# First hundred calls of a hand-ordered attention and MLP kernel in another order, and its filler pieces at another place

## The chip, the cores and the metric

The kernel runs on one core of a Trainium2 chip. Times are device microseconds of one execution; where several runs were timed, their median is given. A profile describes one execution of its own, whose span (first to last instruction) is a little shorter than its time.

## The reference

```python
def _attn_ref(q, k, v, sort_net):        # q, k, v: (4, 8, 768, 64); sort_net: (4, 8, 8, 8)
    P = sort_net
    for _ in range(5):                   # balancing
        P = exp(P - max(P, -1))
        P = P / (sum(P, -1) + 1e-9)
        P = P / (sum(P, -2) + 1e-9)
    k_sorted = einsum('bhij,bhjcd->bhicd', P, k_b)     # 8 blocks of 96 positions
    v_sorted = einsum('bhij,bhjcd->bhicd', P, v_b)
    scores = q_b @ k_sorted^T / 8                      # within each block
    return softmax(scores) @ v_sorted
x = attention output as (3072, 512)
h = x @ w_in                                           # 512 -> 2048
out = (h * cos(h)) @ w_out                             # 2048 -> 512
```

## The kernel before, in words

The work is cut into eight chunks n = 0 to 7, each a half (four blocks of 96 positions) of one of the four batches, with all eight heads. A *unit* (n, u) is one block u = 0 to 3 of a chunk. After the balancing, all calls stand in a list that was written out by hand, `PLAN`. It is read line by line, and each engine executes its own instructions in that order. A letter at the end of a line names the engine that copies (A = ScalarE, V = VectorE) or the PSUM pool (`B` = `big`, three buffers of two banks; `c` = `acc`, two of one bank). A further number is an argument of the call.

The calls that matter here:

- `kp t` (TensorE) makes a third of the sorted keys of the first batch, `kpe t` copies it to SBUF.
- `v0 z` (TensorE) makes an eighth of the sorted values of the first batch (8 of 64 columns), `v0e z` copies it. Groups 0 to 3 read v as it was loaded. Groups 4 to 7 read `vperm`, a copy in another layout, which `vp 32` makes on GpSimd in two instructions of 16 columns each. A product's weights are 128 columns wide where only 96 are needed, so the last product of a 16-column part also reads the beginning of the next part.
- `S n u` (TensorE) makes a unit's scores, `M` takes the maximum, `X` subtracts it (both VectorE), `E` takes the exponential (ScalarE), `TP` transposes it on TensorE, `TE` copies the transpose, `AV` multiplies by the values (TensorE), `N` divides by the sum (VectorE), `XP`/`XE` transpose the result and copy it to `xT`. `QP`/`QE` turn q for the next chunk.
- `U4 h g part`, `C4`, `G4` are the first matmul of the MLP, the cosine and the product for the first chunk, cut by halves of the columns (h = 0 needs units 0 and 1, h = 1 needs 2 and 3). `U n f`, `C`, `G` do the same for later chunks; a third number in `U n f 1` makes the second of its two column groups in two half matmuls each instead of whole ones. `D`, `O`, `W` are the second matmul, the copy and the store.
- `Lw` loads w_out, `Lk` and `Lv` load k and v of the second batch; `kxp`, `z_turned`, `pk2`, `ones` are small GpSimd work.

Ahead of `PLAN` stand the loads, all issued by GpSimd (q of chunk 0 at line 1004, then k of batch 0 at 1005, v of batch 0 at 1006), and the five rounds of the balancing (`normalize`, on VectorE and ScalarE). During these TensorE turns q (`q_twice`, 64 transposes) and otherwise computes *zero products*: `keep_warm` multiplies a zero matrix into a PSUM buffer that is overwritten later. There are 15 of these at the start, then 2, 6, 2 and 4, and some in `PLAN`: where `kp` or `v0` has a last number (`kp 0 B 1`, `v0 0 B 2`), 512 columns each; in `TP` and `AV` of chunk 0, 256 columns each. The first cuts, as many as `MORE` says, divide such a product into up to four pieces along its columns; each piece is an instruction pair of its own (weight load and matmul).

A PSUM buffer is given to a call when the calls that read its former content have been listed; the call then waits for these.

Of the kernel before, what the change touches and what calls it, by code (L numbers as in the profile page):

```python
# [13 lines left out]
ALU = mybir.AluOpType  # L14
AX = mybir.AxisListType

MORE = 70
PLAN = """\
vp 32
kp 0 B 1  # L20
spv
kp 2 B 1
kpe 0 A
kp 1 B
kpe 2 V
v0 3 c 1
kpe 1 A
v0 1 c 1
v0e 3 V
S 0 0 B  # L30
v0e 1 A
v0 4 B 1
M 0 0
v0 5 c 1
Lw 0
Lw 1
v0e 4 A
Lw 2
Lw 3
ones 0  # L40
S 0 1 B
X 0 0
v0e 5 A
v0 6 c 1
M 0 1
E 0 0 0
v0 7 B
S 0 3 B
v0e 6 A
X 0 1  # L50
TP 0 0 c
v0e 7 A
M 0 3
v0 2 c
E 0 1 1
S 0 2 B
X 0 3
kxp 1
v0e 2 A
v0 0 B 2  # L60
TE 0 0 A
M 0 2
kxp 2
v0e 0 A
TP 0 1 c
X 0 2
kxp 0
z_turned 1
E 0 3 2
AV 0 0  # L70
TE 0 1 V
E 0 2 0
TP 0 3 c
N 0 0
Lk 1
AV 0 1
Lv 1
pk2
TE 0 3 A
TP 0 2 B  # L80
N 0 1
XP 0 0 B
TE 0 2 A
QP 1 1 c
XP 0 1 c
QE 1 1 0 V
z_vperm
XE 0 0 A
AV 0 3
AV 0 2  # L90
XE 0 1 V
N 0 3
U4 0 0 0
U4 0 0 1
N 0 2
z_turned 0
p_pads
U4 0 1 0
C4 0 0
QE 1 1 1 V  # L100
U4 0 1 1
G4 0 0
XP 0 3 c
XP 0 2 c
C4 0 1
U4 0 3 0
XE 0 2 V
U4 0 3 1
XE 0 3 A
G4 0 1  # L110
U4 1 2 0
C4 0 3
U4 1 3 0
G4 0 3
U4 1 2 1
U4 1 3 1
C4 1 2
U4 1 1 0
C4 1 3
G4 1 2  # L120
U4 1 1 1
bl2 c
G4 1 3
C4 1 1
U4 0 2 0
U4 0 2 1
sp2
# [260 lines left out]
G 2 5  # L388
kg 11 c
kge 11 A  # L390
U 2 6
S 3 2 c 1
C 2 6
M 3 2 1
# [438 lines left out]
def kernel(  # L833
# [16 lines left out]
    B, H, S, D = q.shape  # L850
# [197 lines left out]
    nc.scalar.activation(early[:], half_pi[:], AF.Exp)  # L1048


    pieces = [MORE]

    def keep_warm(times, t, cols=512):
        for _ in range(times):
            n = 1 + min(3, pieces[0])
            pieces[0] -= n - 1
            for i in range(n):
                c = slice(i * cols // n, (i + 1) * cols // n)
                nc.tensor.matmul(  # L1059
                    t[:, c], warm[:], warm[:, :1].to_broadcast([128, c.stop - c.start]),  # L1060
                    start=True, stop=True)

    keep_warm(15, big.tile([128, 512], FP32, name="idle", tag="big"))


    V, A = nc.vector, nc.scalar
# [31 lines left out]
    E, Q = E_eps[:, :, :nb], Q_eps[:, :nb]  # L1098
# [45 lines left out]
    def idle(times):  # L1144
        keep_warm(times, acc.tile([128, 512], FP32, name="idle", tag="acc"))

    for it in range(5):
        nc.scalar.activation(E, less[:], AF.Exp)
        if it == 0:
            nc.vector.reduce_sum(  # L1150
                maskp.rearrange("p (b e x) -> p b x e", b=2, e=2),
                ident.rearrange("p (b x e j) -> p b x e j", b=2, e=2, j=nb), axis=AX.X)
            A.copy(
                order.rearrange("k (p r) -> k p r", r=QR),
                ident[:blk, :blk].rearrange("k (r p) -> k p r", r=QR))
            q_twice(0)
            q_twice(1)
            keep_warm(2, big.tile([128, 512], FP32, name="idle", tag="big"))
        if it >= 2:
            q_place(it - 2)  # L1160
            if it < 4:
                idle((6, 2)[it - 2])
                q_twice(it)
            else:
                idle(4)
                q_place(3)
        normalize(it, (less if it < 4 else sorted_by)[:])
        if it == 1:
            nc.gpsimd.tensor_copy(held[:B * H], over[2][:, :1])
            for z in range(3):  # L1170
                load_w_in(z)
        if it == 3:
            nc.gpsimd.tensor_copy(held[:B * H], over[3][:, :1])
            load_w_in(3)
            load_q(1)
# [439 lines left out]
    def spv():  # L1615
# [3 lines left out]
        kp=kp, kpe=kpe, kxp=kxp, ks=ks, kse=kse, kg=kg, kge=kge, kswap=kswap, v0=v0, v0e=v0e,  # L1619
# [3 lines left out]
        vp=vp, vp2=vp2, vq=vq, z_vperm=z_vperm, p_pads=p_pads, pk2=pk2, bl2=bl2, sp2=sp2, spv=spv,  # L1623
        ones=ones, z_turned=z_turned, zeros=zeros_between)
    words = {"A": (A,), "V": (V,), "B": (big, "big"), "c": (acc, "acc"), "-": (None,)}
    for line in PLAN.split("\n"):
        name, *args = line.split()
        given = []
        for a in args:
            given += words.get(a) or ((int(a),) if a.isdigit() else (a,))  # L1630
        calls[name](*given)
# [42 lines left out]
```

## Time and profile before

| | |
|---|---|
| median of 3 runs | 236.35 us (236.2 to 237.87) |
| the profiled execution | 236.52 us |
| its span | 234.7 us |
| TensorE (PE) busy | 227.7 us, 97% |
| VectorE (DVE), ScalarE (ACT), GpSimd (POOL) busy | 175.2, 149.1, 93.7 us |
| DMA traffic | 31.01 MB, mean 132 GB/s |
| chain that ended last: PE, DMA | 84%, 7% of the span |

In the profile, PE is TensorE's matmuls and PEld its weight loads. A row of the timeline gives start, length, engine, source line, operation, output and inputs with their shapes, the number of instructions merged into it, and in brackets how long the engine sat idle before it and who released it. A matmul's recorded length includes its way through the array, so matmuls that follow each other overlap. The chain of waits goes back from the last instruction, at each step to what released it. A row of a stretch gives each engine's busy time and, as (xN), the number of its instructions, then the granted TensorE clock, the share of the DMA engines and GB/s.

### The profile page before, as it was taken

What the parts mean: (1) busy time and instruction counts of PE and PEld (TensorE: products, weight loads), DVE (VectorE), ACT (ScalarE), POOL (GpSimd) and SP (SyncE); (2) the same over time, 40 slices, a digit from 0 to 9 for tenths busy, and PEclk for the clock granted to TensorE, in tenths of its full rate; (3) what the DMA queues carried; (4) which work ended last, traced back from release to release, by engine and by line L of the source; (5) the groups of instructions that cost most, each with busy time, mean ns of one, the idle gap of its engine ahead of it and who ended that gap; (6) DMA issues with size and microseconds to landing.
All of it is one profiled execution on the core that took longest, in us unless ns stands there. A gap on an engine that the chain in (4) does not pass through costs nothing.

```text
span 234.7 us, 5734 instructions
## 1 busy us (share of the span) xinstructions
PE 227.7 (97%) x2380; PEld 151.0 (64%) x2380; DVE 175.2 (75%) x291; ACT 149.1 (64%) x198; POOL 93.7 (40%) x117
## 2 busy tenths in 40 slices
PE   8898999999999999999999999999999999999994
PEld 8766799657765566655666558655555596456553
DVE  5757987798898776897778977899487879455530
ACT  3365976657869859883788747666667376526511
POOL 7659998596990095972709000800000000000000
PEclk9999999999999999999999999999999999999999
DMA  5999999796699779996999668953943650341003
GB/s 63 223 195 207 204 207 226 128 216 164 134 102 179 167 138 168 99 218 152 127 158 95 86 104 148 210 83 68 162 159 64 82 175 3 66 125 47 0 0 134
DMA packets 66841, 31.01 MB, mean 132 GB/s; under 512 B 55552, under 2 KB 62336, under 8 KB 66560
## 3 DMA queue, kind: packets, MB, share of 16 engines
q0 software_dynamic: 24048, 13.64, 43.6%
q1 hardware_dynamic: 42480, 16.83, 34.1%
q8 instruction: 18, 0.29, 0.5%
q10 hardware_dynamic: 288, 0.20, 0.3%
q14 instruction: 7, 0.06, 0.1%
HBM read 27.27 MB, written 6.29 MB: 143 GB/s over the span
## 4 chain that ended last, share of the span: by engine, by line
PE 84%; DMA 7%; ACT 3%; POOL 3%; issue 1%; DVE 1%; DVEq 0%; POOLq 0%
PE o L1544 32%; PE h L1499 30%; DMA kv<-in_v_dram 6%; PE h L1522 5%; PE av L1430 3%; POOL vperm L993 2%; PE sc L1320 2%; PE ks L1201 2%; PE xps L1469 2%; PE o L1638 2%; DMA kv<-p_buf 1%; PE vs L1257 1%; PE pps L1406 1%; PE vs L1292 1%; PE sc L1347 1%
## 5 line engine op out<-in xcount | busy, mean ns | idle before, releaser
L1544 PE MATMUL o<-w_out_t,gg 128*128 128x512 bf16 x368 | 87.2, 379 | 0.0
L1499 PE MATMUL h<-xT,w_in_t 128*128 128x384 bf16 (+1 forms) x516 | 78.2, 305 | 0.0
L1511 DVE TENSOR_TENSOR gg<-c,h 128x768 bf16<-128x768 f32 x56 | 53.0, 949 | 19.0 <-ACT c L1505 18.9
L1505 ACT ACTIVATE c<-h,half_pi 128x768 f32<-128x768 f32 x56 | 50.4, 901 | 22.0 <-PE h L1499 20.7
L1499 PEld LDWEIGHTS <-w_in_t 128*128 128x128 bf16 x516 | 47.1, 98 | 22.4 <-DVE xT L1072 0.2
L1544 PEld LDWEIGHTS <-gg 128*128 128x128 bf16 x368 | 33.3, 98 | 33.7 <-DVE gg L1511 0.6
L1379 ACT ACTIVATE p_buf<-s 96x768 bf16<-96x768 f32 x32 | 26.4, 841 | 12.1 <-DVE s L1375 8.0
L1361 DVE TENSOR_REDUCE mx<-sc 96x8 f32<-96x768 f32 (+1 forms) x41 | 31.5, 772 | 3.3 <-PE sc L1333 1.4
L993 POOL COPY vperm<-kv 64x1536 bf16<-64x1536 bf16 (+1 forms) x10 | 28.1, 2853 | 2.5 <-DMA kv<-in_v_dram 2.5
L1375 DVE TENSOR_TENSOR s<-sc,mx 96x384 f32<-96x384 f32 (+1 forms) x33 | 24.1, 733 | 1.2
L1447 DVE TENSOR_TENSOR xn<-av,r 96x512 bf16<-96x512 f32 x32 | 22.0, 687 | 1.1
L943 POOL DMA_DIRECT2D kv<-in_q_dram x24 | 16.0, 681 | 0.8 <-issue 0.5
L1446 DVE RECIPROCAL r<-av 96x8 f32<-96x8 f32 x32 | 6.3, 198 | 8.1 <-PE av L1430 8.0
L1070 ACT CAST kTs<-ks 128x512 bf16<-128x512 f32 (+1 forms) x18 | 11.0, 632 | 2.2 <-PE ks L1201 2.2
L1070 ACT COPY xT<-xps 128x384 bf16<-128x384 bf16 x10 | 4.8, 476 | 11.3 <-PE xps L1469 11.3
L943 POOL DMA_DIRECT2D q_mem<-in_q_dram x16 | 10.7, 685 | 2.8 <-DMA kv<-in_v_dram 2.4
L1070 ACT COPY kv<-o 128x512 f32<-128x512 f32 (+2 forms) x10 | 5.3, 529 | 9.6 <-PE o L1544 7.0
L1059 PEld LDWEIGHTS <-warm 128*128 128x128 bf16 x116 | 9.8, 119 | 2.3 <-DVE half_pi L1042 1.0
L1522 PE MATMUL h<-xT,w_in_t 128*128 128x192 bf16 x128 | 11.1, 246 | 0.0
L1059 PE MATMUL idle<-warm 128*128 128x128 bf16 (+2 forms) x99 | 9.7, 273 | 1.3 <-DVE half_pi L1042 1.0
L1522 PEld LDWEIGHTS <-w_in_t 128*128 128x128 bf16 x128 | 10.4, 98 | 0.0
L1567 POOL CAST held<-q_turned 96x1 f32<-96x1 bf16 x2 | 0.4, 182 | 24.4 <-DMA q_turned<-q_mem 17.0
(120 smaller groups left out, 276.4 us busy)
## 6 DMA issues: line engine op xcount, KB each, us to landing
out_dram<-kv SPq DMA_DIRECT2D x12, 256.0 KB, 2.5
out_dram<-o_s SPq DMA_DIRECT2D x10, 256.0 KB, 3.3
w_in_t<-in_moe_w_in_dram POOLq DMA_DIRECT2D x4, 512.0 KB, 12.4
w_out_t<-in_moe_w_out_dram POOLq DMA_DIRECT2D x4, 512.0 KB, 11.6
kv<-in_k_dram POOLq DMA_DIRECT2D x2, 768.0 KB, 10.0
kv<-in_v_dram POOLq DMA_DIRECT2D x2, 768.0 KB, 13.6
pair<-in_k_dram POOLq DMA_DIRECT2D x2, 768.0 KB, 10.3
kv<-in_v_dram POOLq DMA_DIRECT2D x6, 256.0 KB, 6.1
```

Source lines behind the costliest of these rows:

```text
L943: nc.gpsimd.dma_start(out=q_heads[:, i, :, e], in_=src[:, ih * IC + i, :, e])
L993: nc.gpsimd.tensor_copy(dst, src)
L1070: eng.copy(dst, src)
L1361: nc.vector.reduce_max(mx[:], s_view(n, u, hp), axis=AX.XY if n < 2 else AX.X)
L1375: nc.vector.tensor_tensor(s, sc, mx.to_broadcast(list(s.shape)), op=ALU.subtract)
L1379: nc.scalar.activation(p[:, :, :blk], s_t.pop((n, u)).rearrange("p e h c -> p (e h) c"), AF.Exp, scale=scale)
L1447: nc.vector.tensor_tensor(xn.rearrange("p h e d -> p e h d")[:, e], avv[:, :, :, :D], r[:, e].to_broadcast([blk, e.stop - e.start, H2, D]) ...
L1499: nc.tensor.matmul(o[:, f2, x * w:(x + 1) * w], w_in_t[:, kk, f * 128:(f + 1) * 128], xT[n][:, kk, x * w:(x + 1) * w], start=(kk == 0), st ...
L1505: nc.scalar.activation(c[:], ps["h", n, fp][:, :, :TC], AF.Sin, bias=half_pi[:, 0:1])
L1511: nc.vector.tensor_tensor(gt[n, fp // 2][:, f:f + 2], ps.pop(("c", n, fp))[:], ps.pop(("h", n, fp))[:, :, :TC], op=ALU.mult)
L1522: nc.tensor.matmul(o[:, part, f2 * w:(f2 + 1) * w], w_in_t[:, kk, f * 128:(f + 1) * 128], xT[0][:, kk, h * w:(h + 1) * w], start=(kk == 0) ...
L1544: nc.tensor.matmul(out_ps[n, ts][:], gt[n, q][:, f % 4, ts * 128:(ts + 1) * 128], w_out_t[:, f, :], start=(f == 0), stop=(f == FC - 1))
```

## The change

The first hundred lines of `PLAN` are put into another order. Two zero products are dropped (`kp 2`, `v0 4`), `v0 4` moves directly behind `v0 3`, the scores of units 0 and 1 move ahead of `v0 1` and `v0 5`. `AV 0 2` comes ahead of `AV 0 3`, `XP 0 3` between two parts of `U4`, and some C4 and G4 change places. One later line, `U 2 6`, is split. The number of cuts `MORE` becomes two numbers: 18 before and during the balancing, 52 from the start of `PLAN`; a zero product of 512 columns is now cut into up to five pieces, one of 256 into up to three.

```diff
-MORE = 70
+MORE = 18,52
 PLAN = """\
-vp 32
 kp 0 B 1
 spv
-kp 2 B 1
+kp 2 B
+kp 1 B
+vp 32
 kpe 0 A
-kp 1 B
+v0 3 c 1
+v0 4 B
+kpe 1 A
 kpe 2 V
-v0 3 c 1
-kpe 1 A
+S 0 0 B
+v0e 3 V
 v0 1 c 1
-v0e 3 V
-S 0 0 B
+v0e 4 A
+S 0 1 B
 v0e 1 A
-v0 4 B 1
+Lw 0
 M 0 0
+X 0 0
 v0 5 c 1
-Lw 0
+E 0 0 0
 Lw 1
-v0e 4 A
 Lw 2
 Lw 3
+S 0 3 B
+v0e 5 A
 ones 0
-S 0 1 B
-X 0 0
-v0e 5 A
+M 0 1
 v0 6 c 1
-M 0 1
-E 0 0 0
+v0e 6 A
 v0 7 B
-S 0 3 B
-v0e 6 A
 X 0 1
-TP 0 0 c
 v0e 7 A
 M 0 3
+E 0 1 1
 v0 2 c
-E 0 1 1
 S 0 2 B
-X 0 3
 kxp 1
+TP 0 0 c
 v0e 2 A
 v0 0 B 2
 TE 0 0 A
+v0e 0 A
+X 0 3
 M 0 2
...
 TE 0 2 A
 QP 1 1 c
+QE 1 1 0 V
+XP 0 0 B
+XE 0 0 A
 XP 0 1 c
-QE 1 1 0 V
 z_vperm
-XE 0 0 A
+XE 0 1 V
+AV 0 2
+N 0 2
 AV 0 3
-AV 0 2
-XE 0 1 V
-N 0 3
+z_turned 0
 U4 0 0 0
 U4 0 0 1
-N 0 2
-z_turned 0
+C4 0 0
 p_pads
+N 0 3
 U4 0 1 0
-C4 0 0
 QE 1 1 1 V
+XP 0 3 c
+G4 0 0
 U4 0 1 1
-G4 0 0
-XP 0 3 c
+C4 0 1
 XP 0 2 c
-C4 0 1
+XE 0 2 V
 U4 0 3 0
-XE 0 2 V
 U4 0 3 1
+G4 0 1
 XE 0 3 A
-G4 0 1
 U4 1 2 0
+U4 1 3 0
 C4 0 3
-U4 1 3 0
+U4 1 2 1
...
-U 2 6
+U 2 6 1
...
-    pieces = [MORE]
+    pieces = [MORE[0]]
 
     def keep_warm(times, t, cols=512):
         for _ in range(times):
-            n = 1 + min(3, pieces[0])
+            n = min(1 + pieces[0], max(3, cols // 102))
             pieces[0] -= n - 1
...
     words = {"A": (A,), "V": (V,), "B": (big, "big"), "c": (acc, "acc"), "-": (None,)}
+    pieces[0] = MORE[1]
     for line in PLAN.split("\n"):
```

More of the change, by code (lines that the diff above doesn't have):

```diff
@@ L61 @@
 TE 0 0 A
+v0e 0 A
+X 0 3
 M 0 2
+E 0 3 2
 kxp 2
-v0e 0 A
+kxp 0
 TP 0 1 c
 X 0 2
-kxp 0
+AV 0 0
 z_turned 1
-E 0 3 2
-AV 0 0
 TE 0 1 V
@@ L73 @@
 TP 0 3 c
+Lk 1
+Lv 1
 N 0 0
-Lk 1
 AV 0 1
-Lv 1
+N 0 1
 pk2
@@ L80 @@
 TP 0 2 B
-N 0 1
-XP 0 0 B
 TE 0 2 A
 QP 1 1 c
+QE 1 1 0 V
+XP 0 0 B
+XE 0 0 A
 XP 0 1 c
-QE 1 1 0 V
 z_vperm
-XE 0 0 A
+XE 0 1 V
+AV 0 2
+N 0 2
 AV 0 3
-AV 0 2
-XE 0 1 V
-N 0 3
+z_turned 0
 U4 0 0 0
 U4 0 0 1
-N 0 2
-z_turned 0
+C4 0 0
 p_pads
+N 0 3
 U4 0 1 0
-C4 0 0
 QE 1 1 1 V
+XP 0 3 c
+G4 0 0
 U4 0 1 1
-G4 0 0
-XP 0 3 c
+C4 0 1
 XP 0 2 c
-C4 0 1
+XE 0 2 V
 U4 0 3 0
-XE 0 2 V
 U4 0 3 1
+G4 0 1
 XE 0 3 A
-G4 0 1
 U4 1 2 0
+U4 1 3 0
 C4 0 3
-U4 1 3 0
+U4 1 2 1
+C4 1 2
+U4 1 3 1
+C4 1 3
 G4 0 3
-U4 1 2 1
-U4 1 3 1
-C4 1 2
 U4 1 1 0
-C4 1 3
+U4 1 1 1
+C4 1 1
+bl2 c
 G4 1 2
-U4 1 1 1
-bl2 c
 G4 1 3
-C4 1 1
 U4 0 2 0
```

## The prediction

> **What bounds the kernel now.** I read the page first, then the chain of waits in order of time, then the instructions of single engines around the changed calls.
>
> ```profile
> span 234.7 us, 5734 instructions
> ...
> PE 227.7 (97%) x2380; PEld 151.0 (64%) x2380; DVE 175.2 (75%) x291; ACT 149.1 (64%) x198; POOL 93.7 (40%) x117
> ...
> PEclk9999999999999999999999999999999999999999
> ```
>
> TensorE (PE) is busy for 97% of the span and its granted clock never shows less than 9 tenths. Once it streams, only less work or an earlier start can help. The chain of waits (start, us, what) says where the start is set:
>
> ```profile
> 2.74 12.95 DMA kv<-in_v_dram
> 15.74 5.55 POOL vperm L993 x2
> 21.34 0.20 PE vs L1257
> 21.54 0.22 PE sc L1333 x14
> ...
> 25.42 0.87 PE vs L1257 x8
> 26.32 0.58 ACT vS L1070
> 26.90 0.75 ACT p_buf L1379
> 27.69 0.56 PE pps L1406 x8
> ...
> 30.61 0.26 PE av L1430 x8
> 30.87 2.68 PE h L1522 x32
> ...
> 98.16 1.30 PE h L1499 x8
> ```
>
> The load of v lands at 2.74 + 12.95 = 15.69. GpSimd's two copies `vp 32` run until 21.29, and from there the chain passes through the last product of `v0 5`, the scores, `v0 0`, its copy, two exponentials and transposes to the first matmul of the MLP, `U4 0 0 0`, at about 30.75. Behind that TensorE is nearly gapless to the end, so what the kernel gains or loses is what that start gains or loses. What stands around it on TensorE:
>
> ```profile
> 14.21 0.39 PE L1059 MATMUL ks<-warm 128*128 128x512 bf16 x1
> 14.54 0.64 PE L1201 MATMUL ks<-bd,kv 64*128 64x64 bf16 x16
> 15.11 0.39 PE L1059 MATMUL ks<-warm 128*128 128x512 bf16 x1
> 15.43 1.10 PE L1201 MATMUL ks<-bd,kv 64*128 64x64 bf16 x32
> 16.46 0.39 PE L1059 MATMUL vs<-warm 128*128 128x512 bf16 x1
> 16.79 0.91 PE L1257 MATMUL vs<-bdv,kv 64*128 64x192 bf16 x8
> ...
> 19.02 0.39 PE L1059 MATMUL vs<-warm 128*128 128x512 bf16 x1
> 19.34 0.59 PE L1257 MATMUL vs<-bdv,vperm 64*128 64x128 bf16 x8
> 19.86 0.39 PE L1059 MATMUL vs<-warm 128*128 128x512 bf16 x1
> 20.18 0.56 PE L1257 MATMUL vs<-bdv,vperm 64*128 64x128 bf16 x7
> 21.34 0.20 PE L1257 MATMUL vs<-bdv,vperm 64*128 64x64 bf16 x1 [0.59 <-POOL vperm L993]
> ```
>
> The eighth product of `v0 5` waits for the second copy (its 128 columns reach into it), and the scores `S 0 1` are queued behind it in TensorE's order. VectorE and ScalarE pay for that:
>
> ```profile
> 19.13 0.95 DVE L1361 TENSOR_REDUCE mx<-sc 96x8 f32<-96x768 f32 x1 [0.71 <-PE sc L1333]
> 20.12 0.95 DVE L1371 TENSOR_TENSOR s<-sc,mx 96x768 f32<-96x768 f32 x1
> 21.81 0.95 DVE L1361 TENSOR_REDUCE mx<-sc 96x8 f32<-96x768 f32 x1 [0.74 <-PE sc L1333]
> ...
> 26.58 0.95 DVE L1371 TENSOR_TENSOR s<-sc,mx 96x768 f32<-96x768 f32 x1
> ...
> 30.26 0.34 DVE L1072 COPY xT<-xps 128x384 bf16<-128x384 bf16 x1
> ```
>
> From `M 0 1` at 21.81 VectorE runs almost without a gap to `XE 0 1`, which ends at 30.60 and is one of the two things that `U4 0 0 0` waits for. The other is the transpose copy `TE 0 2` on ScalarE: behind it `AV 0 3` and `AV 0 2` still run, in the chain to 30.87.
>
> **Why v lands at 15.69.** These are rows of the DMA-queue view: the whole span, then 11.5 to 12.6, 13.15 to 13.6 and 13.6 to 14.2. The last fence has the busy time of the engines up to 11.6 and from there to 19.3.
>
> ```profile
> q8 instruction: 18, 0.29, 0.5%
> ```
> ```profile
> q8 instruction: 1, 0.02, 5.4%
> ```
> ```profile
> DMA packets 38, 0.03 MB, mean 73 GB/s; under 512 B 6, under 2 KB 38, under 8 KB 38
> ```
> ```profile
> DMA packets 108, 0.12 MB, mean 193 GB/s; under 512 B 6, under 2 KB 107, under 8 KB 107
> ```
> ```profile
> 0.00:11.60 11.60, 9.60 (x143) 9.07 (x143) 7.41 (x34) 4.22 (x9) 8.43 (x18) 1.00 0.82 143
> 11.60:19.30 7.70, 7.45 (x124) 5.17 (x121) 3.94 (x12) 4.06 (x6) 5.22 (x5) 1.00 1.14 198
> ```
>
> Queue q8 carries 18 packets of 0.29 MB / 18 = 16 KB. Against 2 x 2380 instructions of TensorE that is one packet for about 256: these are fetches of its program. The first comes between 11.5 and 12.6, when 286 instructions have run, the second at 19.3 after 531. It takes 5.4% of 16 engines for 1.1 us, so 0.95 us of one engine. At that time all 16 engines stream k and v, whose packets are the only ones over 8 KB. Of those none starts from 13.15 to 13.6, and exactly one starts after 13.6 (108 less 107). I read this as the engine that had to fetch, with its last piece of v late. The landing waits for it.
>
> **The change, part by part.**
>
> *Pieces.* Before, 70 cuts go to the first products: 60 fills, then 8, 24, 3 and 4 during the balancing, 99 in all. Now it is 4 x 5 + 3 + 10 = 33, then 2, 6, 2, 4, in all 47. The columns are the same, and those phases wait for a load or for VectorE, so their length costs nothing. But with 64 transposes of q, TensorE now issues 2 x (47 + 64) = 222 instructions before the matmuls of `block`, 254 after them, 286 in the middle of `kp 0`. The fetch therefore starts between about 14.1 and 14.9, not 11.6, when every piece of v has begun. The landing of v gains at least 13.60 - 13.15 = 0.45 and at most the fetch's 0.95 (at worst nothing: a rival). I take 0.75: v lands at 14.94, `vp 32` runs 14.99 to 20.54, its first copy to 17.77. [...]
>
> *Fills.* Two are gone, those of `kp 2` and `v0 4`. A fill takes 0.32 to the next product (14.21 to 14.54) and 0.12 to get going behind 64-row products (15.43 + 1.10 less 0.20 for the last one's own length, then 16.46), so some 0.4 each. Seven remaining 512-column fills become five pieces: 0 to 0.06 each; I take 0.02. The 256-column ones stay as long. `U 2 6 1` makes eight half matmuls out of four: 2.68 / 32 = 0.084 each against 1.30 / 8 = 0.163 for a whole one, so 0.02 in all.
>
> *The order on TensorE*, with product times from the rows above. `kp 0` as before to 15.03; `kp 2` and `kp 1` directly behind it to 15.96 (16.37 before); fill and `v0 3` to 17.1. Now `v0 4` stands here and waits for the first copy, 17.77 + 0.06 = 17.83: 0.7 idle, in which `S 0 0` is held although its keys are ready at about 17.2. Then: `v0 4` 0.40, `S 0 0` 0.23, fill 0.46, `v0 1` 0.69, `S 0 1` 0.27, fill 0.46, `v0 5` 0.40. This is 20.74, past the second copy's 20.54, so `v0 5` waits no more. Then `S 0 3` 0.23, fill and `v0 6` 0.86, `v0 7` 0.42, `v0 2` 0.78, `S 0 2` 0.38 (it takes a buffer that `v0e 7` frees), `TP 0 0` with fill 0.55, two fills and `v0 0` 1.33. The last product of `v0 0` starts at 25.3; before it started at 26.06 (the chain's 25.42 + 0.87, less drain). That is 0.8 gained.
>
> *VectorE.* `M 0 0` starts 0.23 behind `S 0 0`, at 18.7 (19.13), `X 0 0` at 19.7, `M 0 1` at 20.55 directly behind it instead of 21.81, and the row of equal operations follows 1.2 earlier up to `X 0 2`. *ScalarE* limits: `v0e 0` starts with the 0.8 gained, then `E 0 3`, `E 0 2`, `TE 0 3` and `TE 0 2` follow at their old durations. `AV 0 2` now goes first, with its fill already run while it waits: another 0.1. `U4 0 0 0` starts 0.9 earlier, at 29.85; `XE 0 1`, 1.05 earlier, is no longer late.
>
> *Behind it.* `XP 0 3` moves between two U4 parts and takes a buffer that `XE 0 1` has freed; its `N 0 3` ends some 0.4 before. `U4 1 3 0` ahead of `C4 0 3`, and the exchanged C4/G4, leave TensorE fed: each C4 waits for its own U4 part alone. On GpSimd and SP nothing changes order, and no queue is passed: the `Lw` issues follow `vp 32` as before. The q load's issue on GpSimd, and its time to landing from the DMA-queue view between 12.6 and 14.2:
>
> ```profile
> 12.85 0.79 POOL L933 DMA_DIRECT2D q_mem<-in_q_dram  x1
> ...
> q_mem<-in_q_dram POOLq DMA_DIRECT2D x1, 384.0 KB, 14.8
> ```
>
> The loads that queue up on GpSimd are paced by the DMA engines and land as before. The nearest is the q of `QP 1 1`: issued at 12.85, it lands 14.8 later at 27.65, and `QP 1 1` now starts at 28.2 (29.2 before), still 0.5 behind it. Sum: -0.9 at `U4`, +0.02 for `U 2 6 1`: **-0.9 us**. The profiled execution took 236.52 (span 234.7 and 1.8 around it), so it would take 235.6. The runs' median is 236.35, which gives **235.5**.
>
> **Rivals.** *The landing does not move* (the late piece of v is late for another reason, or the fetch strikes again). Then `v0 4` stands idle until 18.52 + 0.06, `S 0 0` comes 0.3 later than now, but `S 0 1` still runs ahead of `v0 5`; `v0 0` gains only 0.1 and `AV 0 2` 0.1. 236.1. For it: only one packet's lateness speaks for my reading. Against it: its size fits 0.95.
>
> *Gained and given back*: the start is early, but a later stage waits for a transfer that is not. 236.35. Against it: the chain holds 7% DMA, and nearly all of that is the first load.
>
> *The clock falls: slower than before.* The 0.7 idle, with two fills fewer, might make the gate lower the granted clock. The start shows the price, as products of 128 columns in two stretches:
>
> ```profile
> 1.00:5.90 4.90, 4.90 (x47) 1.00 0.67 77
> 5.90:6.70 0.80, 0.80 (x16) 1.00 1.66 307
> ```
>
> 9.6 per us at first, then 20: half speed for 4.9 us. Falling once while TensorE has dense work costs half of that, 2.45: 235.5 + 2.45 = **238.0**. It decides from the stall before `v0 4` onwards. Against it: 0.59 idle at 20.75 (the row of 21.34) did not move the PEclk row. [...]
>
> *The change does not do what it says.* That can only be half so: the scores stand earlier in TensorE's order whatever becomes of the fetch, and the half that can fail, the pieces, is the first rival.
>
> **How the numbers follow.** My forecast, 235.5 with a range of its own from 235.1 (v lands 0.95 earlier, and nothing else is late) to 235.9 (0.45), has 0.62. The landing that stays (236.1) has 0.16, given back (236.35) 0.11, the slower clock (238.0) 0.05, a larger gain than the sum (up to 1.5, if VectorE's whole 1.2 comes through and the pieces cost nothing: 234.8) 0.06. The range 234.8 to 236.6 leaves out the clock and little else. A measurement of this kernel can tell about 1%, 2.4 us, from no change; all but the clock's case lie within it. Faster by over 1%: 0.03; within 1%: 0.91; slower by over 1%: 0.06.
>
> **What would show it.** Right: the fetch's packet after 14; no packet over 8 KB starting after 13.6; `vperm` starting near 15.0; TensorE idle for 0.7 before `v0 4`, released by GpSimd; `M 0 1` directly behind `X 0 0`; `U4` from about 29.85, and the same distance from there to the end (234.7 - 30.75 = 203.95). Wrong: `vperm` still near 15.7 (the fetch was not the cause, then 236.1), a wait of `QP 1 1` for its load, a new wait of PE between 30 and 60, or fewer than 9 tenths in PEclk.

## The result, and the profile after

The changed kernel takes 235.29 us (median of 11 runs, 235.07 to 235.77); the kernel before took 236.4 beside it (11 runs, 235.81 to 237.87). The ratio is 0.9944, 95% interval 0.9929 to 0.9959: 1.1 to 1.3 us faster, of which the forecast of 235.5 had 0.9. The sum came out nearly right, but not by its own steps: the start gained more than predicted, and a part of that was lost again later.

The page of the profile after, which took 235.77 us, the longest of its runs:

```profile
span 234.0 us, 5701 instructions
...
PE 224.7 (96%) x2353; PEld 148.5 (63%) x2374; DVE 175.3 (75%) x291; ACT 149.1 (64%) x198; POOL 93.9 (40%) x117
...
PEclk9999999999999999999999999999999999999999
```

As before, TensorE's clock holds and it is busy nearly throughout (2353 of its 2374 matmuls were recorded). The DMA queues between 13.6 and 14.2 us, then the chain of waits (start, us, what):

```profile
DMA packets 119, 0.13 MB, mean 224 GB/s; under 512 B 3, under 2 KB 118, under 8 KB 118
...
q8 instruction: 1, 0.02, 10.1%
```
```profile
2.74 11.74 DMA kv<-in_v_dram
14.53 2.79 POOL vperm L993
17.37 0.59 PE vs L1258 x8
...
29.07 0.26 PE av L1431 x8
29.33 1.98 PE h L1523 x24
...
59.23 4.75 DMA kTs<-kTs
64.11 0.50 PE sc L1321 x8
...
102.97 3.22 DMA kv<-p_buf
106.23 0.43 PE av L1431 x8
```

The one packet over 8 KB that starts there (119 less 118) is the fetch itself: every piece of v is under way by then. v lands at 2.74 + 11.74 = 14.48, 1.21 earlier than before. The chain reaches the MLP's first matmuls at 29.33 (30.87 before, 1.54 later). Two links further down were not in the chain of before in this form: the key swap of the second batch, which now takes 4.75, and a longer `kv<-p_buf` (2.87 before). TensorE and VectorE at the places that the prediction named:

```profile
16.40 0.92 PE L1258 MATMUL vs<-bdv,kv 64*128 64x192 bf16 x8
17.37 0.51 PE L1258 MATMUL vs<-bdv,vperm 64*128 64x128 bf16 x6
...
29.17 0.50 PE L1523 MATMUL h<-xT,w_in_t 128*128 128x192 bf16 x4
```
```profile
64.11 0.50 PE L1321 MATMUL sc<-kTs,q_turned 128*128 128x96 bf16 x8 [0.52 <-DMA kTs<-kTs]
```
```profile
18.23 0.95 DVE L1362 TENSOR_REDUCE mx<-sc 96x8 f32<-96x768 f32 x1 [0.19 <-PE sc L1334]
19.22 0.95 DVE L1372 TENSOR_TENSOR s<-sc,mx 96x768 f32<-96x768 f32 x1
20.09 0.94 DVE L1362 TENSOR_REDUCE mx<-sc 96x8 f32<-96x768 f32 x1
```

`v0 4` starts at 17.37 with hardly a pause behind `v0 3` (16.40 + 0.92 is 17.32, of which the last product's own recorded length, from 17.10 on, is 0.22), `M 0 1` follows `X 0 0` without a gap at 20.09 (21.81 before), `U4 0 0 0` starts at 29.17 instead of 30.75, 1.58 earlier. But the profiled execution as a whole is only 236.52 - 235.77 = 0.75 us shorter: 0.83 us of the 1.58 is given back, and the scores behind the key swap at 64.11, before which TensorE stands for 0.52, are one place of it.

All kernels that were run, each with one profiled execution. "U4" is the first row of `h` in its chain of waits; the column behind it is the span less that start. The medians and ratios leave out executions whose mean granted clock was below 0.98 (the last column counts them; they took 241 to 245 us) but keep those of e3 and e12 with 0.986 to 0.993, save that the ratio of e12 also leaves out its slowest, of 241.34.

| kernel | v lands | U4 | U4 to end | profiled, us | median, us | ratio to before, 95% | clock < 0.98 |
|---|---|---|---|---|---|---|---|
| before | 15.69 | 30.87 | 203.9 | 236.52 | 236.3 to 236.6 | 1 | 0 |
| after | 14.48 | 29.33 | 204.6 | 235.77 | 235.29 | 0.9944 (0.9929 to 0.9959) | 0 of 11 |
| after, again (e8) | 14.11 | 29.13 | 204.2 | 235.06 | 235.06 | 0.9939 (0.9916 to 0.9961) | 0 of 6 |
| pieces alone (e1) | 13.88 | 30.21 | 204.9 | 236.9 | 236.2 | 0.9994 (0.9979 to 1.0008) | 0 of 12 |
| order alone (e2) | 15.28 | 30.03 | 204.7 | 236.52 | 236.01 | 0.9979 (0.9956 to 1.0002) | 7 of 12 |
| new order, no cuts (e3) | 13.95 | 28.93 | 209.7 | 240.38 | 237.89 | 1.0063 (1.0033 to 1.0094) | 0 of 12 |
| new order, 40 cuts ahead (e4) | 14.69 | 29.56 | 204.4 | 235.86 | 236.41 | 1.0 (0.9975 to 1.0025) | 5 of 12 |
| order alone, two fills back (e5) | 15.38 | 30.10 | 204.1 | 236.01 | 235.98 | 0.998 (0.9964 to 0.9995) | 1 of 12 |
| after without the split (e6) | 14.26 | 29.36 | 204.7 | 235.88 | 235.3 | 0.995 (0.9932 to 0.9967) | 0 of 10 |
| e3 with 15 splits (e7) | 14.20 | 28.94 | 205.3 | 236.04 | 235.38 | 0.995 (0.9931 to 0.9969) | 0 of 8 |
| after, `vperm` later (e9) | 13.90 | 29.82 | 204.7 | 236.34 | 235.92 | 0.9967 (0.9948 to 0.9987) | 4 of 12 |
| after, a `D` ahead (e10) | 14.21 | 29.13 | 205.2 | 236.1 | 234.74 | 0.992 (0.9892 to 0.9949) | 0 of 6 |
| e7 with that `D` ahead (e11) | 13.88 | 28.93 | 203.7 | 234.45 | 234.45 | 0.9903 (0.9878 to 0.9929) | 0 of 6 |
| before, no cuts (e12) | 13.97 | 30.12 | 209.5 | 241.34 | 239.55 | 1.0097 (1.0059 to 1.0135) | 0 of 6 |

### The profile page after: what moved, and what is told of

It is laid out like the page before. It is cut to its first block, busy times and chain, and to the rows that moved or that the text cites. A ratio compares the mean times of both kernels' runs of the same rounds, so it can differ in the third digit from the quotient of the medians.

```text
span 234.0 us, 5701 instructions
## 1 busy us (share of the span) xinstructions
PE 224.7 (96%) x2353; PEld 148.5 (63%) x2374; DVE 175.3 (75%) x291; ACT 149.1 (64%) x198; POOL 93.9 (40%) x117
## 4 chain that ended last, share of the span: by engine, by line
PE 80%; DMA 10%; ACT 3%; issue 2%; POOL 2%; DVE 1%; SPq 0%; DVEq 0%; ACTq 0%; POOLq 0%
PE h L1500 30%; PE o L1545 29%; DMA kv<-in_v_dram 5%; PE h L1523 5%; PE av L1431 3%; PE sc L1321 2%; DMA kTs<-kTs 2%; PE vs L1258 2%; PE o L1640 2%; PE xps L1470 2%; DMA kv<-p_buf 1%; DMA pT<-p_buf 1%; PE ks L1202 1%; POOL vperm L993 1%; PE pps L1407 1%
## 5 line engine op out<-in xcount | busy, mean ns | idle before, releaser
L1545 PE MATMUL o<-w_out_t,gg 128*128 128x512 bf16 x348 | 84.2, 379 | 1.1 <-issue 0.3
L1060 PE MATMUL idle<-warm 128*128 128x512 bf16 (+4 forms) x46 | 9.0, 364 | 2.2 <-ACT q_turned L1143 1.1
L1060 PEld LDWEIGHTS <-warm 128*128 128x128 bf16 x106 | 7.7, 111 | 5.4 <-issue 2.7
```

Of the source, the lines that this page charges most:

```text
L1545: nc.tensor.matmul(out_ps[n, ts][:], gt[n, q][:, f % 4, ts * 128:(ts + 1) * 128], w_out_t[:, f, :], start=(f == 0), stop=(f == FC - 1))
```

## The experiments

### The two halves of the change (e1, e2)

e1 keeps the old order and takes the new cuts; e2 takes the new order and split with the old cuts:

```diff
 e1, against before:                    e2, against after:
-MORE = 70                              -MORE = 18,52
+MORE = 18,52                           +MORE = 70,0
 (and the new rule for n in keep_warm,   (and the old rule for n in keep_warm)
  with the second number from PLAN on)
```

> The old order of calls and the old fills; only the cuts are as in the new kernel (18 ahead of the list, 52 in it, up to five pieces). Theory (the fetch of TensorE's program delays one sixteenth of v): the first fetch comes at about 14 instead of 11.6, v lands at 14.5 to 14.9 instead of 15.7, v0 5 waits no more for the second copy of vperm, U4 starts 0.6 to 0.8 earlier than before; with a few tenths given back later, 235.8 to 236.0. Rival (the new order does it): v lands near 15.7, 236.4 as before.

> The new order of calls and the new fills; only the cuts are as in the kernel before (70, at the first products, up to four pieces, none left for the list). Theory: the first fetch is back at about 11.6 and v lands near 15.7; TensorE idles over 1 us before v0 4, and U4 starts only 0.1 to 0.3 earlier than before: 236.1 to 236.3. Rival (the order does it): v lands near 15.7 or not, 235.3 as the new kernel.

Measured: the fetch moves with the cuts, not with the order. In e1 it comes at 14.06 and v lands at 13.88; in e2 it comes at 11.49 and v lands at 15.28, its last sixteenth 1.35 behind the fifteenth (13.93). Waits of e2, first in its chain, then on TensorE:

```profile
2.74 12.54 DMA kv<-in_v_dram
15.34 2.78 POOL vperm L993
...
30.03 1.98 PE h L1523 x24
```
```profile
18.17 0.51 PE L1258 MATMUL vs<-bdv,vperm 64*128 64x128 bf16 x6 [0.87 <-POOL vperm L993]
```

With the late landing TensorE does stand before `v0 4`, for 0.87. At U4 each half is worth something, 0.66 in e1 and 0.84 in e2, and together they make 1.50, about what the whole change shows. For e2 that is far more than the 0.1 to 0.3 expected, and the falls of the clock in seven executions (taken up at e5 and e9) were not expected. At the end neither half alone is worth it: e1's interval holds 1, e2's just does, and e1's median of 236.2 is above its expected 235.8 to 236.0. What e1 gains at the start it loses at two transfers. Its chain of waits, and the DMA view between 108.2 and 110.9 us (the digits are the busy share of the 16 DMA engines in 40 slices):

```profile
106.07 5.06 DMA pT<-p_buf
111.18 0.43 PE av L1430 x8
...
136.43 4.54 DMA xT<-xn
```
```profile
DMA  9521019888899610000000000000001000010000
...
q8 instruction: 1, 0.02, 3.7%
...
xT<-xn SPq DMA_TRANSPOSE x1, 4.3
```

A program fetch starts at 108.64, 2.57 behind the issue of a transposing transfer that is still running, lasts for 1.61 us, and from 109.3 on the DMA engines move next to nothing for 1.6 us. The transpose `pT<-p_buf` takes 5.06 where it takes 2.94 in the profile before, `xT<-xn` behind it 4.3 instead of 2.33. The same happens at 138.54 to the `xT<-xn` issued at 136.43. The kernel before has a fetch in that transfer too (at 138.45; it takes 3.84), so there e1 loses only the difference, 0.70. This gave the **theory of the fetches**: a fetch that falls into a transfer on which the chain depends makes it longer (here by 2.12 for the `pT<-p_buf`), and where it falls follows from how many instructions TensorE has been given before.

### How many cuts, and where (e3, e4)

```diff
 e3, against after:   e4, against after:
-MORE = 18,52        -MORE = 18,52
+MORE = 0,0          +MORE = 40,52
```

> The new kernel without any cut: every zero product is one instruction pair. Theory (only the number of instructions ahead of the first fetch counts): the first fetch comes at about 15, v lands at 14.5, the start of U4 and the time are those of the new kernel, 235.2 to 235.5. Rival (the cuts in the list do something of their own, for the clock or for the weight loads behind them): 0.3 or more slower than the new kernel, or fewer than 9 tenths of the clock granted.

> The new kernel with 40 cuts ahead of the list instead of 18 (55 first products instead of 33). Theory: 256 instructions have run at about 12.4, so the first fetch comes near 12.9, when the last piece of v has begun on every engine: v lands at 14.5 to 14.9 and the time is that of the new kernel within 0.2. Rival (each instruction moved behind the balancing helps a little): half way between the order alone and the new kernel, 235.7 to 235.9.

e4 misses in the fetch's place: it comes at 11.23, inside the load, not where the count of instructions put it; the landing is 14.69 and U4 at 29.56. It misses in the time too: 236.41, not that of the kernel after. Its profiled execution (235.86) is its fastest, so where the others lose more is not shown. The count tells the place of a fetch only roughly: the first one comes behind 286 instructions of TensorE in before and behind 244 in after, so that no run shows the expectation's 256 as the count at which it starts, and the eleventh one comes behind 2778 in before and behind 2708 in e1, which has as many ahead of it. e3 refutes the expectation that missing cuts cost nothing. Its start is earlier than after's (28.93 against 29.33), and it is slower than before by 0.6%. Its chain and TensorE around 105 us, then two stretches (the number behind POOL's is the granted clock):

```profile
28.93 1.98 PE h L1523 x24
...
102.04 5.83 DMA kv<-p_buf
107.91 0.65 PE av L1431 x8
108.56 5.90 PE o L1545 x16
```
```profile
104.43 0.20 PE L1348 MATMUL sc<-kTs,q_turned 64*128 64x96 bf16 x1
107.25 0.47 PE L1348 MATMUL sc<-kTs,q_turned 64*128 64x96 bf16 x7 [2.61 <-DMA kTs<-kTs]
```
```profile
104.50:107.20 2.70, 0.13 (x1) 0.03 (x1) 1.47 (x2) 0.20 (x1) 0.00 (x0) 0.88 1.23 88
107.20:108.00 0.80, 0.56 (x9) 0.35 (x9) 0.24 (x1) 0.00 (x0) 0.00 (x0) 0.50 1.11 241
```

The fetch that the kernels before and after and e1, e2 and e4 have between 94.5 and 98.6 comes at 104.34 here, in the key swap of the next batch. The swap is late, TensorE stands for 2.61 us, and its clock falls to half: the same 16 matmuls of `o` take 5.90 instead of the 3.45 to 3.46 of before and after. The fall is only a part of the loss: seven of the twelve executions keep their clock (1.0) and still take 236.9 to 238.0.

### Is it the number of instructions? (e7, e12)

If so, putting the missing instructions back at another place must cure e3, and taking the cuts out of the kernel before must spoil it. e7 splits all of `U 1 0` to `U 2 7`, 8 instructions for each split; e12 is before without cuts:

```diff
 e7, against e3:                            e12, against before:
-U 1 0                                     -MORE = 70
+U 1 0 1                                   +MORE = 0
 (and so on to U 2 7: 15 splits in all,
  U 2 6 is split already)
```

> The new order without any cuts, as in the run of 237.89, but with all of U 1 0 to U 2 7 split (15 more, 120 instructions for the 124 of the missing cuts): the start stays as early (U4 near 28.9), the program fetches from about 97 us on come where they come in the kernel after (97 to 98, 109 to 112, 137 to 138) and not at 104.3, inside the key swap. Theory of the fetches: the stall of 2.6 us at 104.5 and the fall of the clock behind it go away, no execution over 239, median 235.0 to 235.7 (start 0.24 earlier than after, splits +0.3). Rival (the cuts do something of their own, whatever the fetches do, or the early start itself is what runs into the swap): still 237 to 238, with the stall at 104 to 107.

> The kernel before, in its old order, without any cuts (70 pairs, 140 instructions fewer at the start). Theory of the fetches: the first fetch comes at about 17.5, v lands at 13.9 to 14.2 and U4 starts 0.5 to 0.8 earlier than before's 30.75; but from then on all fetches come 140 instructions later, one of them at 104 to 105 inside the key swap as in the new order without cuts, TensorE waits there for 1 to 3 us, and the time is 237 to 239, slower than before, in spite of the earlier start. Rival (that stall belongs to the new order or to its start at 28.9, not to the number of instructions): 235.5 to 236.3, and no wait of over 0.5 us at 104 to 107.

Both came out as the theory of the fetches said, and against its rivals. e7: 235.38 instead of 237.89 with the same start, and its fetch back at 98.13. e12 is slower than before by 0.97% (239.55, a little over the 237 to 239 expected) although its U4 starts 0.75 earlier; its fetch comes at 105.11. Its chain, TensorE's wait, and two stretches:

```profile
103.23 5.44 DMA kv<-p_buf
108.72 0.65 PE av L1430 x8
109.37 4.83 PE o L1544 x16
```
```profile
108.05 0.33 PE L1347 MATMUL sc<-kTs,q_turned 64*128 64x96 bf16 x7 [2.37 <-DMA kTs<-kTs]
```
```profile
108.00:110.00 2.00, 1.61 (x17) 0.92 (x17) 1.49 (x2) 0.00 (x0) 0.00 (x0) 0.65 0.97 194
110.00:112.00 2.00, 2.00 (x6) 0.76 (x5) 1.22 (x3) 0.84 (x1) 0.93 (x3) 0.50 0.59 176
```

The second part of this swap takes 6.78 in e3 and 6.81 in e12, with the fetch in it, and 5.05 to 5.70 in the twelve other profiles. That is not the whole delay: in e3 it lands 1.86 later than in e7, of which 1.09 is its length and 0.77 a later issue, whose cause is not shown.

So the cuts, of which I said that their length costs nothing, do matter, by the instructions that they add ahead of everything else.

### The split, and the kernel after again (e6, e8)

```diff
 e6, against after:
-U 2 6 1
+U 2 6
```

> The kernel after with U 2 6 unsplit: eight instructions fewer on TensorE from about 97 us on, so each later program fetch comes some 0.6 us later (111.0 to about 111.6, 137.6 to 138.2). My sum put the split at +0.02: 235.3, range 235.0 to 235.6. Theory of the fetches (where one falls into a transposing transfer that the chain waits for, 0.4 to 2.6 us are lost): the fetch near 111 stays clear of the pT and xT transfers (which end at 109.3) and so the time stays too, unless the one near 138 takes the xT transfer issued at 135.9 from off the path to on it: then 235.6 to 236.0.

> The kernel after once more, for a second profile beside the others. Theory of the fetches: where a fetch falls varies with the execution, so the wait of 0.52 us for the key swap at 64.1 (fetch at 59.23, 1.44 us long) is absent in most executions; a profile near the median of 235.3 shows U 1 without it, a swap of about 3.7 instead of 4.75, and the end 1.2 to 1.3 earlier than before's. Rival (the wait belongs to the kernel): it is there again, and the profile stands at 235.3 for another reason, found elsewhere.

The split alone moves nothing that these runs resolve (235.3 against 235.06 and 235.29). e8's execution is at the median of its six runs, and the wait of after's first profile is absent:

```profile
63.23 0.72 PE L1321 MATMUL sc<-kTs,q_turned 128*128 128x96 bf16 x8
```

The fetch came at nearly the same moment as in after (59.30 against 59.23), but lasted 0.92 and not 1.44, and the swap's second part took 3.47 instead of 4.75. All 14 profiles fall in line here: without a fetch in it (e3, e7, e11, e12) this part takes 2.98 to 3.02, with a fetch of 0.88 to 0.96 (before, e1, e4, e5, e8) 3.47 to 3.73, with one of 1.33 to 1.44 (after, e2, e6, e9, e10) 4.21 to 4.75. So this wait hangs on the execution: the 0.52 of the first profile of after is absent in the second, and in e6, e9 and e10 TensorE stands there for 0.25, 0.34 and 0.38 (in e6 released by a copy on ScalarE). Without it e8 gives back 0.28 of the 1.74 that it has at U4. Why a fetch lasts longer in one execution than in another is not shown.

### The executions in which the clock falls (e5, e9)

e5 puts the two dropped zero products back into e2; e9 makes `vperm` later in after, without another instruction on TensorE:

```diff
 e5, against e2:     e9, against after, in vp(lo):
-kp 2 B             +early = vperm[slice(0, 64), :CD].rearrange("p (d c) -> p d c", d=D)
+kp 2 B 1           +nc.gpsimd.tensor_copy(early[:, lo:lo + 5], vv[slice(0, 64), lo:lo + 5, :blk])
-v0 4 B
+v0 4 B 1
```

> The order alone with the 70 cuts as before, and the two dropped zero products back (kp 2 and v0 4): TensorE has 0.8 us more to do while it waits for vperm (idle before v0 4 0.87 us in the profile of the order alone). Theory A (the executions of the order alone that take 240.9 to 243.6, with a mean clock of 0.955 to 0.972, lose their clock in the stall before v0 4 when v lands late): the idle time there falls to about 0.1, no execution over 239, median 235.6 to 236.2. Theory B (they lose it later, where a program fetch falls into a transposing transfer that TensorE waits for, as in the run without cuts, where 2.61 us idle at 104.5 to 107.2 was followed by half the clock up to 113): the stall at the start is no matter, and between a quarter and two thirds of the executions still take 240 or more. Either way U4 starts near 30.0.

> The kernel after with the first 5 of vperm's columns copied twice, so that GpSimd's first copy is done some 0.87 us later (5/16 of 2.79) and TensorE stands idle before v0 4 for about 1.1 us instead of 0.2, as long as in the profile of the order alone (0.87); its instructions, and so its program fetches, stay as they are. Theory A (the executions of 240 and more, with a mean clock of 0.955 to 0.972, which the order alone and the forty cuts show, lose their clock in that stall): a part of the executions, 2 to 7 of 12, take 239 to 245. Theory B (they lose it elsewhere): no execution over 239. In both the others take 235.6 to 236.2, the U4 start 0.7 to 0.87 later than after's.

The counts speak for theory A on both sides: with cover the count goes from 7 of 12 to 1 of 12 (theory A said none), and a later `vperm` alone brings 4 of 12 (240.9 to 244.1) into a kernel that had none in 17. In the new order, the four kernels whose profile shows a wait before `v0 4` (0.87 in e2, 0.51 in e9, 0.26 in e4, 0.25 in e5) are the four that have such executions; the other seven had none in 59. But the counts do not follow the length of the wait (5 of 12 in e4, 1 of 12 in e5), and the waits were other than expected (about 1.1 for e9, 0.1 for e5). No execution with a fallen clock was profiled, so that the clock falls in this wait is not shown, nor why the times come in two groups (about 241 and 244); and e9 also makes GpSimd's later issues some 0.85 later than in e8.

The two fills themselves were worth little: e5's U4 starts at 30.10, e2's at 30.03, against some 0.4 for each in my sum. In front of a late `vperm` they are hidden.

### A place at which most versions pay, and a faster version (e10, e11)

Between 102 and 117 us after, e8 and e2 each lose 0.36 to 0.57 of their lead. TensorE waits there for two transfers in a row, the swap and `kv<-p_buf`; the kernel before, whose chain goes through `kv<-p_buf` too, waits for that one alone (so does e1, which loses nothing there). Before, e8, then e7:

```profile
106.97 0.43 PE L1430 MATMUL av<-vS,kv 96*128 96x65 bf16 x8 [0.34 <-DMA kv<-p_buf]
```
```profile
104.89 0.33 PE L1348 MATMUL sc<-kTs,q_turned 64*128 64x96 bf16 x7 [0.20 <-DMA kTs<-kTs]
105.51 0.43 PE L1431 MATMUL av<-vS,kv 96*128 96x65 bf16 x8 [0.30 <-DMA kv<-p_buf]
```
```profile
105.38 0.33 PE L1348 MATMUL sc<-kTs,q_turned 64*128 64x96 bf16 x7 [0.73 <-DMA kTs<-kTs]
106.04 0.43 PE L1431 MATMUL av<-vS,kv 96*128 96x65 bf16 x8 [0.33 <-DMA kv<-p_buf]
```

e10 and e11 list a part of the second matmul, which is ready, ahead of both:

```diff
+D 2 1 1
 T 4 0 B
 vge 0 8 A
 AV 3 1
 hp 3 3
 Lq 5
-D 2 1 1
```

> The kernel after with D 2 1 1 (0.86 us of TensorE) listed ahead of T 4 0 and AV 3 1, which in all the profiles wait there for the key swap and for kv<-p_buf (0.20 + 0.30 us in the second profile of after, 0.42 in that without the split): if the 0.36 us that every version gives back between 102 and 117 is that wait, the profile shows no TensorE wait there and an end that is 0.3 earlier: 234.8 (234.5 to 235.0), some 0.3 below after's 235.06 to 235.29. If the wait only moves to what follows (AV 3 2 for the pT transfer, M 4 0 which comes up to 0.4 later): 235.1 to 235.3, no change.

> The new order without cuts and with the 15 splits (235.38; it lost 0.94 between 102 and 117, with 0.74 + 0.33 us of waits for the same two transfers, and 0.5 at 140 for an xT transfer with a fetch in it), with D 2 1 1 ahead in the same way. If those waits are the loss, 0.5 to 0.8 comes back: 234.6 to 234.9, below the kernel after. If the queue's lateness is only passed on: 235.2 to 235.5.

e11 takes 234.45, 0.97% below before, with an interval that ends where e7's begins (0.9929 and 0.9931). It is the fastest kernel here, and the only one whose start comes through whole (U4 to end 203.7, 203.9 before). Of the 1.59 between the profiled executions of e7 and e11, 1.10 is won at this place, the rest between 137 and 152 us. Its chain has no transfer there any more:

```profile
28.93 1.98 PE h L1523 x24
...
104.26 0.34 PE vs L1285 x16
104.60 0.97 PE o L1545 x4
105.57 0.28 PE sc L1348 x8
105.85 0.38 PE av L1431 x8
```

e10's median of 234.74 points the same way, but its interval overlaps after's, and its profiled execution is its slowest (236.1, the others up to 234.87). There `kv<-p_buf` took 4.73, and TensorE still waits for 0.45 and 0.47, though the `D` ahead of it fills about 1.0:

```profile
106.59 0.33 PE L1348 MATMUL sc<-kTs,q_turned 64*128 64x96 bf16 x7 [0.45 <-DMA kTs<-kTs]
107.39 0.43 PE L1431 MATMUL av<-vS,kv 96*128 96x65 bf16 x8 [0.47 <-DMA kv<-p_buf]
```

## Why the prediction was right, and where it was not

**The time** was right, at 235.29 for 235.5, by two errors of opposite sign: -1.58 instead of -0.9 at U4, and +0.83 in the profile instead of nothing behind it. That they nearly cancel is luck.

**The fetch delays v.** Right, in both directions (e1, e2). It came at 14.00, just ahead of the forecast 14.1 to 14.9. The "about 256" instructions to a packet were my estimate: 4760 / 18 is 264, and in the profile before the 18 fetches start 247 instructions apart on average (188 to 319). Four profiles with the first fetch at 11.2 to 11.7 have v landing at 15.69, 15.28, 14.69 and 15.38 (mean 15.26); the ten with it at 14 or later at 13.88 to 14.48 (mean 14.08). **The size was wrong**: 1.2 and not 0.75. My upper bound, the fetch's own 0.95, was no bound: the last sixteenth lies 1.35 behind the fifteenth in e2 and in e5 (15.38 against 14.03), and why by more than the fetch lasts is not shown. The rival that the landing stays is refuted by e1.

**The order on TensorE.** The term of the idle time before `v0 4` was mis-sized: 0.7 predicted, next to none in the profile. The first copy came 0.45 earlier than I had it (17.32 against 17.77), and `v0 3` ended at 17.32 and not at 17.1. `M 0 0` at 18.23 and `M 0 1` at 20.09 are both 0.46 to 0.47 ahead of the forecast, and the step that `M 0 1` follows `X 0 0` directly held. To U4 it grows to 0.68 (29.17 against 29.85). Whether the dropped fills are worth 0.4 each no run tells: e5 has them in front of a late `vperm`, where they are hidden.

**"Nothing is given back"** is the step that failed. I held U4's distance to the end for constant, because the chain of before was nearly all TensorE there. That meant only that most transfers came just in time: 1.5 us earlier, the swaps and `kv<-p_buf` come last. At one place even that was not so, for `kv<-p_buf` stands in the chain of before, with a wait of 0.34. The rival *gained and given back*, at 0.11, is half of what happened: the wait of 0.52 in some executions (64 us, the key swap with a long fetch in it) and 0.36 in both profiles of the kernel after (102 to 117 us), less a few hundredths won elsewhere. For the second place e11 shows that the wait for the two transfers was the cause. My argument against the rival, that the chain holds 7% DMA, counted the transfers that ended last and not those that were nearly last.

**The split**: +0.02, and no difference measured.

**The clock falls.** Not in the changed kernel, none of whose 17 runs were below 0.99. But beside it, with the same order and a later `vperm`, executions lose 5 us and more (e2, e4, e9), so in this order the early v may matter twice; that it is the wait before `v0 4` is argued and not shown. The price of 2.45 fits one of the two falls that could be read: 5.90 - 3.46 for `o` and 0.65 - 0.43 for `av` make 2.66 in e3, 4.83 - 3.46 and 0.65 - 0.43 make 1.59 in e12. The executions that lose 5 us and more cost twice the price, so 238.0 was too low for them.

## What to carry to other kernels

A gain at the start was worth here what the transfers behind it let through: the 1.94 us that e11 has at U4 came through whole, while the profile after lost 0.83 of its 1.58. So list, for each wait for a transfer later on, by how little it is met now, and put ready work ahead of it before moving the start. Instructions that cost no time of their own moved the later fetches of TensorE's program: without the cuts the one between 94.5 and 98.6 came at 104.34, in the key swap, and the median was 2.60 above that of after (e3). So in a kernel like this one count instructions, and look at where each fetch falls. One profile showed a wait that another of the same kernel did not have (0.52 at 64.11 in after, none there in e8), so profile a kernel twice before explaining a difference of half a microsecond.

## What the runs showed of the hardware

*A transposing transfer took longer with a program fetch beside it.* In the 14 profiles there are 154 transfers `xT<-xn`. In the 107 without a fetch running between 0.6 and 2.35 us behind their issue, they take 2.28 to 2.42 us (median 2.35); in the 47 with one, 2.97 to 4.54 (median 3.84). The two groups don't overlap; in the profiles before and after alone they are 16 of 2.28 to 2.42 and 6 of 3.24 to 4.30. For `pT<-p_buf`, with fetches up to 2.6 us behind the issue, the medians are 2.94 (87) and 4.16 (11), and the groups overlap (up to 3.36 without, from 2.80 with). The 36 fetches in the profiles before and after last 0.88 to 1.53 us each.

*Behind two waits of 2.4 to 2.6 us TensorE's clock was at half*: in e3 (2.61) the granted clock is 0.88 over the 2.7 us of the wait and 0.50 right behind it, in e12 (2.37) 1.00 from 105.6 to 108, 0.65 from 108 to 110 and 0.50 from 110 to 112; in the profiled executions with waits of 0.87 (e2), 0.73 (e7) and 0.51 (e9) the mean granted clock is 1.0. Which wait is just long enough is not shown.
